# Clustered attention and a mixture of causal-attention experts in one program: a second emission order for the same recorded operations

## The chip, the cores and the metric

The kernel runs on one core of one Trainium2 chip. The metric is the device time of one launch in microseconds (us). Engines are named as in the profile: PE is the matrix engine (PEld are its weight loads), DVE the vector engine, ACT the scalar engine, POOL the GpSimd engine, and SP the engine that issues nearly all DMAs of this kernel.

## The reference

The first part is attention within clusters, for 4 batches of 8 heads, 768 positions and 64 dimensions. The second part takes the result as x (4 x 768 x 512), picks two of four experts for each position, and adds the experts' causal attentions with the weights of the gate.

```python
q_n = q / (np.linalg.norm(q, axis=-1, keepdims=True) + 1e-06)      # k_n, c_n alike
q_assign = np.argmax(np.einsum('bhsd,hcd->bhsc', q_n, c_n), axis=-1)   # 16 clusters; k_assign alike
mask = q_assign[:, :, :, None] == k_assign[:, :, None, :]
scores = np.where(mask, scale * np.matmul(q, k.transpose(0, 1, 3, 2)), -1000000000.0)
x = softmax(scores) @ v                     # heads side by side: (4, 768, 512)
...
logits = x @ w_gate                         # 4 experts, the 2 largest kept, softmax over them
for e in range(E):
    q, k, v = x @ wq[e], x @ wk[e], x @ wv[e]
    a = softmax(np.where(causal, -1000000000.0, scale * (q @ k.transpose(0, 2, 1))))
    ye = a @ v @ wo[e]
    out += (weight of e at this position, 0 if not picked) * ye
```

## The kernel before

The work is cut into 24 steps. The first 16 are head pairs of the first part (4 batches by 4 pairs); the last 8 are expert pairs of the second part (4 batches by 2 pairs). In time the first part fills about 0 to 400 us, with the second part's first steps overlapping its end.

A head pair runs as follows. k, q and v are loaded; PE transposes k and q (L516) and multiplies them with the normalized centroids (L547); DVE finds the cluster of each position and writes it as a row of zeros and ones (L559 to L567); from these come "rows" that are appended to the operands of the score matmuls, so that pairs of different clusters get a large negative score. Operands are split into a rounded part `hi` and a rest `lo = x - hi` to keep precision, and both are carried by DMA into the tiles `tk` (k side) and `tq` (q side). Score maxima come from matmuls at L1055 and DVE reductions at L1061; their negatives, `mr`, also go by DMA into `tq`. Scores (L1134 to L1143) are exponentiated by ACT (L1153); PE multiplies them with v (L1191). The sums of the softmax are collected by POOL or DVE: elementwise sums of 128x768 tiles (L375 on POOL, L376 on DVE), and then a matmul with ones (L1215). The sums `ssb` make a round trip through DRAM: `sd<-ssb`, `r<-sd`, a reciprocal on DVE (L1243), `rd<-r`, and `rb<-rd`, which spreads them over 64 partitions. With `rb` the result is normalized into `xt` (L1266) and stored as x.

An expert pair runs alike, with projections of x (L773, L813; copies by ACT at L819 and L820), the gate on DVE (L834 to L842, with one exponential on ACT at L844 and the rest at L848 to L852), causal maxima (L970 to L986), exponentials (L1017) and the out projection (L1305).

Every engine executes its instructions in the order in which they were emitted, and all transfers named here stand in the one queue of SP, issued at L358. An instruction that waits holds up everything behind it on its engine. The order is neither that of the Python loops nor chosen by a scheduler at run time: all 3726 operations are first recorded in a `Plan`, and `Plan.run` emits them in the order of a table of numbers, `SEQ`; a letter behind a number moves the operation to the other engine that can do it (a: ACT, d: DVE, p: POOL). `SLOT` says which of the buffers of a name each tile takes. The durations that stand in the `op(...)` calls are not used when the program is emitted.

```python
        for word in SEQ.split():
            i = int(word.rstrip("adp"))
            o = self.ops[i]
            eng = self.LETTER.get(word[-1], o.eng)
            ...
            o.ways[eng][1]()
```

While PE has no work at the start, 37 calls of `spin` (placed by `SEQ` as well) issue matmuls whose result nobody reads, at L1332 and L1327. I call them fillers.

Of the kernel before, what the change touches and what calls it, by code (L numbers as in the profile page):

```python
# [10 lines left out]
def _warn_once_fixed(msg, *args, **kwargs):  # L11
# [26 lines left out]
418 5 25 3 7 24 64 13 6 20 22 32 21 18 34 16 30 10 40 45 41 46 49 50 51 52 53 37 38 42d 55 43 47 56 57 19 1 29 27  # L38
231 234 232 233 222 227 223 12 228 394 69 44p 48p 70 246 68 67 39 58 59 235d 60 61 225d 0 36 62 63 66 65 26 28 395
77 78 79 224 226p 31 71 11 237 4 33 229 230p 238 239 8 80 81p 14 9 397 82p 403 17 399 401 73 84 396 72 74 83 54 76p  # L40
75p 566 249 85 398p 400 402p 23 2 88 15 96 108 94 92 35 240 241 109 97 104 242 243 89 421 93 404 405 406 407 106 244
245 247 422 248 100 409 410 90 102 86 105 101 111 114 115 107 87 95 136 256 103 257 134 98 173 174 99 91 110 163 164
168 169 157 158 252 137 253 152 116 117 138 153 112 113 254 255p 258 260 261 250 423 575 259p 262 135 139 130 131
# [3 lines left out]
302 265 292 293 279 280 303 290 291 430 431p 426 432 427p 434 433 236 251 184 185 189 182 183 310 195 196 188 190  # L47
193 199 267 268 273 202 311 277 278 203 308 309 207 208 204 578 579 266 300 306 296 283 284 194 210 211 274 307 301
287 297 312 313 314d 315 447 448 460 461 445 576 577 437 438 468 449 446 450 457 469 472 571 572 573 567 568 439 440
435 473 436 209 212 213 178 179 581 474 475 453 454 569 570p 574p 478 353 479 470 471 458 582 583 584 585 354 339  # L50
# [3 lines left out]
605 379 380 480 377 319 466 320 481 467 484 321 328d 376d 333d 338d 343d 347 348 378 381 742 743 744 745p 738 739  # L54
740 741p 349 350 382 945 923 459 485 631 628 629 486 487 749 645 620 635 747 646 750 383 909 218 219 748 633 616 617
639 612 613 634 621 636 351 352d 752 753 384 503 649 385 386 954 763 387 765 764 650 651 754 652 632 640 501 546 516
# [3 lines left out]
514 766 767 768 770 771 772 773p 774 946 656 657d 658 947d 775 388 389 1116 580 507 521 522 505 510d 548d 769 776  # L60
552 553 554 555 948d 951d 952 390 972 674 675 802 803 804 785 786 805 779 789 955 956 780 665 666 667 957 958 659
810 811 824 795 796 825 799 800 790 814 815 679 787 680 960 961 515 520 523 524 556 557 962 781 782 662 816 817 677
678 660 818 819 696 687 661 688 663 777 664 788 963 964 698 668 699 700 669 822 697 670 672 673 701 682 783 720 721
702 703 715 716 965 784 823 966 778 808 683 722 812 806 807 809 813 820 710 821 826 723 967 968 689 690 797 798 953p
949p 973 971 712 713 1117 1121 791 1122 792 793 671 1125 751 558 974 975 391 676 681 684 685 794 801 717 707 708 970
969 1287 559 392d 705 718 978 979 976d 1118d 980 686d 981 704d 706 709d 982 983 827 692 693 711 725 726 977 828d 829
560 561 221 562 564 563 984 833 1003 839 1128 1129 840 834 841 1126 991 1123 1124p 1119d 1142 714d 719d 724d 727
691d 694 1127d 1131 1132 1028 835 1004 695d 728 1120 1296 729 1144 565 922 992 843 844 1022 1023 1029 830 1032 1033
# [137 lines left out]
        "7301746154621553250067046341503275432707130341722002261416574140212631230256766304524377512365417302",  # L206
    vt="010101010101010100101100001110",
    mx="0101010110011001010110101010100101010101",
    ssb="010101010101010101101010",
    acc="010101010101011010011001101010011010",  # L210
    avu="010101010101010101100110",
    r="0101010101010101010101010",
    xt="0100110010110001010011100101000111011",
# [1186 lines left out]
```

## Time and profile before

| | |
|---|---|
| three timed runs, us | 683.66, 685.24, 685.85 (median 685.24) |
| profiled execution, us | 684.16 |
| its span, us | 682.3 |
| busy: PE | 666.6 us (98%) |
| busy: DVE | 518.4 us (76%) |
| busy: POOL | 355.1 us (52%) |
| busy: ACT | 341.0 us (50%) |

The span reaches from the first to the last recorded instruction; the profiled execution took 1.9 us more than it. The profiled execution lies 1.08 us under the median of the timed runs. A PE that is "busy" may have matmuls in flight behind each other, so 98% is not 98% of its peak. The granted clock of PE was 1.00 in every stretch shown below.

### The profile page before, as it was taken

To read this page: it belongs to the slowest core of one execution; us is meant where nothing else is said; L and a number is where in the kernel's file an instruction comes from. 1 tells how busy PE (TensorE), PEld (TensorE's weight loads), DVE (VectorE), ACT (ScalarE), POOL (GpSimd) and SP (SyncE) were. 2 spreads that over 40 slices of the span, in tenths; PEclk is the share of its full clock that TensorE was granted. 3 is DMA by queue.
4 is the path that set the end of the run, shared out by engine and by line. 5 is a ranking of instruction groups with operands and counts; after the bars stand their busy time and mean duration, and the time that the engine had idled before them with its cause. 6 is when DMAs were issued, how large, how long until landed. Compare 5 with 4: busy or idle time off the path is not lost.

```text
span 682.3 us, 13483 instructions
## 1 busy us (share of the span) xinstructions
PE 666.6 (98%) x4831; PEld 519.2 (76%) x4831; DVE 518.4 (76%) x1179; ACT 341.0 (50%) x789; POOL 355.1 (52%) x308
## 2 busy tenths in 40 slices
PE   8999999899999999999999999999899999999998
PEld 6777588477686677687686688969879979868976
DVE  6997779789896898889988966666856588656462
ACT  4556466356464475464684553254334434424613
POOL 7496476153888764753578467148431322642200
PEclk9999999999999999999999999999999999999999
DMA  6877757777667768658576631413011130114123
GB/s 187 209 195 170 181 131 176 202 177 202 163 162 205 175 183 205 153 152 220 141 192 163 172 104 48 118 57 110 24 55 42 49 83 30 57 41 141 47 73 124
DMA packets 70734, 90.78 MB, mean 133 GB/s; under 512 B 21088, under 2 KB 60428, under 8 KB 70668
## 3 DMA queue, kind: packets, MB, share of 16 engines
q1 hardware_dynamic: 70524, 89.90, 49.8%
q8 instruction: 38, 0.62, 0.4%
q14 instruction: 28, 0.23, 0.1%
q10 hardware_dynamic: 144, 0.03, 0.0%
HBM read 36.54 MB, written 12.91 MB: 72 GB/s over the span
## 4 chain that ended last, share of the span: by engine, by line
PE 84%; DVE 5%; DMA 4%; POOL 2%; SPq 2%; ACT 1%; issue 1%; POOLq 0%; DVEq 0%; ACTq 0%
PE banks L1191 19%; PE banks L773 10%; PE banks L1055 9%; PE banks L1134 8%; PE banks L1135 7%; PE banks L1003 6%; PE banks L813 5%; PE banks L1305 5%; PE banks L1215 2%; PE banks L516 2%; PE banks L970 2%; PE banks L547 2%; SPq L358 2%; PE banks L1138 1%; PE banks L1143 1%; POOL wvh L375 1%
## 5 line engine op out<-in xcount | busy, mean ns | idle before, releaser
L1061 DVE TENSOR_REDUCE mx<-banks 128x1 f32<-128x384 f32 x384 | 190.0, 548 | 18.9 <-PE banks L1055 17.9
L1055 PE MATMUL banks<-tk,tq 80*128 80x384 f32 x384 | 112.4, 359 | 2.5 <-DVE avu L371 1.1
L1134 PE MATMUL banks<-tq,tk 128*128 128x384 f32 x324 | 113.4, 350 | 0.0
L1135 PE MATMUL banks<-tq,tk 97*128 97x384 f32 x324 | 109.7, 339 | 0.0
L1055 PEld LDWEIGHTS banks<-tk,tq 80*128 80x128 f32 x384 | 68.3, 189 | 13.9 <-issue 4.4
L1153 ACT ACTIVATE p<-banks 128x384 f32<-128x384 f32 x144 | 65.8, 498 | 25.1 <-PE banks L1135 15.8
L1134 PEld LDWEIGHTS banks<-tq,tk 128*128 128x128 f32 x324 | 61.3, 189 | 4.3 <-issue 0.6
L1135 PEld LDWEIGHTS banks<-tq,tk 97*128 97x128 f32 x324 | 61.6, 190 | 0.0
L375 POOL TENSOR_TENSOR acc<-acc,p 128x768 f32<-128x768 f32 (+1 forms) x25 | 43.7, 1746 | 30.9 <-DVE M L1065 9.8
L978 DVE CUSTOM_DVE_ANT_0 banks<-banks,tri 128x384 f32<-128x384 f32 (+4 forms) x96 | 46.0, 529 | 10.7 <-PE banks L970 10.3
L1191 PE MATMUL banks<-p,vt 128*64 128x384 f32 x288 | 50.2, 490 | 0.0
L370 ACT ACTIVATE avu<-banks 128x384 f32<-128x384 f32 x35 | 16.9, 489 | 64.9 <-PE banks L1191 59.5
L375 POOL TENSOR_TENSOR lo<-xk,hi 128x384 fp32r<-128x384 f32 x28 | 28.4, 1026 | 36.3 <-DMA tq<-lo 22.7
L1153 ACT ACTIVATE xl<-banks 128x384 f32<-128x384 f32 x88 | 41.6, 498 | 8.1 <-PE banks L1135 5.6
L1003 PE MATMUL banks<-tk 64*128 64x384 f32 (+2 forms) x432 | 44.5, 312 | 0.0
L1153 ACT ACTIVATE xh<-banks 128x384 f32<-128x384 f32 x80 | 38.3, 499 | 7.9 <-PE banks L1135 7.3
L1266 POOL TENSOR_TENSOR xt<-avu,rb 128x384 f32<-128x384 f32 x28 | 28.3, 1021 | 23.6 <-DMA rb<-rd 23.6
L1191 PEld LDWEIGHTS banks<-p,vt 128*64 128x64 f32 x288 | 20.1, 137 | 24.5 <-issue 21.3
L1003 PEld LDWEIGHTS banks<-tk 64*128 64x128 f32 x432 | 35.4, 185 | 1.6 <-ACT p L1017 0.5
L1191 PE MATMUL banks<-xl,vt 128*64 128x384 f32 x176 | 30.7, 488 | 0.0
L375 POOL TENSOR_TENSOR wvh<-wvh,p 128x768 f32<-128x768 f32 x13 | 24.3, 1866 | 11.6 <-DVE wvh L376 10.4
L1017 ACT ACTIVATE tq<-banks 128x768 f32<-128x768 f32 (+2 forms) x41 | 26.4, 670 | 4.8 <-PE banks L1003 4.2
(322 smaller groups left out, 1682.0 us busy)
## 6 DMA issues: line engine op xcount, KB each, us to landing
tk<-hi SPq DMA_DIRECT2D x60, 192.0 KB
tq<-hi SPq DMA_DIRECT2D x56, 192.0 KB
rb<-rd SPq DMA_DIRECT2D x46, 192.0 KB
vt<-in_v_dram SPq DMA_DIRECT2D x16, 384.0 KB
x<-xt SPq DMA_DIRECT2D x16, 384.0 KB
kt<-in_k_dram SPq DMA_DIRECT2D x15, 384.0 KB
qt<-in_q_dram SPq DMA_DIRECT2D x15, 384.0 KB
tk<-lo SPq DMA_DIRECT2D x30, 192.0 KB
```

Source lines behind the costliest of these rows:

```text
L375: ways = [("pool", t_pool(n), lambda: POOL.tensor_tensor(dst(), a(), b(), op=fn)), ("dve", t_dve(n), lambda: DVE.tensor_tensor(dst(), a(), ...
L773: PE.matmul(m()[:, :HW], w_()[:, dc, es], x_[dc]()[:, js], start=(i == 0), stop=(i == 3 * DC - 1))
L813: PE.matmul(m()[:, :NV], x_[dc]()[:, ts], w_()[:, dc, :], start=(i == 0), stop=(i == 3 * DC - 1))
L978: DVE.tensor_tensor_reduce(ps()[:, h, :w], ps()[:, h, :w], tri[:, 512 - w:], 1.0, -3.0e38, OP.add, OP.max, to)
L1003: PE.matmul(p()[:, h, o_:HW], kone[0][r] if a is None else a()[r, ks], b()[r, qs], start=(j == 0), stop=(j == 3))
L1055: PE.matmul(ps()[:, :w], Q[0:R, 0, h, c * 128:(c + 1) * 128], K[0:R, 0, h, i * w:(i + 1) * w], start=True, stop=True)
L1061: DVE.tensor_reduce(mx()[:, h, cc, i:i + 1], ps()[:, :w], axis=AX.X, op=OP.max)
L1134: PE.matmul(p()[:, o_:HW], K[:, 1, h, ks], Q[:, 1, h, qs], start=True, stop=False)
L1135: PE.matmul(p()[:, o_:HW], K[0:R, 0, h, ks], Q[0:R, 0, h, qs], start=False, stop=True)
L1153: ACT.activation(pt()[:, h, po:po + w], p()[:, o_:HW], AF.Exp, scale=SC)
L1191: PE.matmul(av()[h * 64:(h + 1) * 64, o_:HW], d["vv"](h, kc), pt()[:, h, po:po + HW - o_], start=(kc == 0), stop=(kc == nk - 1), tile_posi ...
L1305: PE.matmul(m()[:, :n1 - n0], a_()[:, ts], w_()[:, ep, n0:n1], start=(ep == 0 and i == 0), stop=(ep == EP - 1 and i == 2))
```

## The change

The operations that are recorded, the buffers and the transfers stay. What differs is the table `SEQ` (all of it), the tables `SLOT` for ten of the names, the planner's numbers in the `op(...)` calls of DMAs (which the emission does not use), and `spin`:

```diff
@@ SEQ
-418 5 25 3 7 24 64 13 6 20 22 32 21 18 34 16 30 10 40 45 41 46 49 50 51 52 53 37 38 42d 55 43 47 56 57 19 1 29 27
...
+23 15 64 0 14 5 4 32 28 40 45 46d 47d 48p 41 43 27 6 37 38 42d 49 50 51 52 1 13 53 55 56 12 57 231 234 25 232 20 222
...
-        o = op("sp", 2 * [(0.58, 1.05, 0.04)], go, t1 + 7, sums, [ssb])
+        o = op("sp", 2 * [(0.58, 1.05, 0.12)], go, t1 + 7, sums, [ssb])
...
-    filled = [0]
...
     def spin():
-        filled[0] += 1
-        if filled[0] in (22, 31):
-            a, w = (identf, identf) if filled[0] == 31 else (blk[:, 0], blk[:, 1])
-            for i in range(8):
-                j, n = i % 6 * 66, 65 if a is identf else 66
-                PE.matmul(idle()[:, j:j + n], a, w[:, :n], start=True, stop=True)
-        elif filled[0] in (23, 32, 33):
-            pass
-        else:
-            for _ in range(2):
-                PE.matmul(idle()[:, :256], onesb, onesb[:, None, :].to_broadcast([128, 2, 128]), start=True, stop=True)
+        for _ in range(2):
+            PE.matmul(idle()[:, :256], onesb, onesb[:, None, :].to_broadcast([128, 2, 128]), start=True, stop=True)
```

So the fillers are 74 matmuls of 256 columns instead of 64 of these and 16 smaller ones. Ahead of the first transposes of k stand 16 of them, where 32 stood.

Counted over the whole program, the choice of engines moves too: sums of 128x768 are 118 on DVE instead of 95, and 96 on POOL instead of 119. The copies are split between ACT and DVE nearly as before.

The order moves nearly everywhere, by small steps. Three places are shown, with the rows of one engine each.

First, SP's queue where, in the trace of before, the time is about 118 to 136 us. The numbers behind a name tell tiles apart; `tk_98`, `tq_97` and `tq_99` are operand tiles of the scores. Before:

```order
L358 DMA qt_1514<-in_q_dram 128x2x384
L358 DMA vt_1516<-in_v_dram 128x2x384
L358 DMA sd<-ssb_1383 4x1x192 x2
L358 DMA tk_98<-rows_1483 16x4x384
L358 DMA tq_99<-rows_1483 16x4x384
L358 DMA kt_1540<-in_k_dram 128x2x384
L358 DMA r_1542<-sd 128x12
L358 DMA tq_99<-hi_1550 64x2x384 x4
L358 DMA tq_97<-mr_1595 1x12x128
L358 DMA rd<-r_1542 128x12
...
L358 DMA rb_1602<-rd 64x768 x2
L358 DMA tq_99<-lo_1555 64x2x384 x2
```

and the same step of the program after the change:

```order
L358 DMA sd<-ssb_1344 4x1x192 x2
L358 DMA qt_1354<-in_q_dram 128x2x384
L358 DMA tk_98<-hi_1302 64x2x384 x4
L358 DMA vm_1332<-in_moe_wq_dram 128x4x64
L358 DMA tk_98<-lo_1365 64x2x384 x2
L358 DMA r_1509<-sd 128x12
...
L358 DMA tq_99<-hi_1535 64x2x384 x4
L358 DMA rd<-r_1509 128x12
L358 DMA tq_97<-mr_1550 1x12x128
L358 DMA tq_99<-lo_1547 64x2x384 x2
L358 DMA vt_1562<-in_v_dram 128x2x384
L358 DMA rb_1611<-rd 64x768 x2
```

The store `sd<-ssb` moved ahead of the load of q, the load of v moved behind the whole piece, eight DMAs instead of three stand between `sd<-ssb` and `r<-sd`, and `tq<-lo` moved ahead of `rb<-rd`.

Second, ACT's queue at the first gate of the second part (about 482 to 491 us before). L844 is the exponential of the gate; L1017 are exponentials of scores. Before:

```order
L1017 ACTIVATE tq_5474<-banks 128x2x256
L1017 ACTIVATE p_0_5484<-banks 128x2x128
L1017 ACTIVATE p_0_5484<-banks 128x2x256
L844 ACTIVATE sm_5503<-sm_5503 128x6
L1017 ACTIVATE tq_5474<-banks 128x2x128
L1220 ACTIVATE ssb_5540<-banks,eps 128x192
```

and after the change:

```order
L819 ACTIVATE lg_5376<-banks 128x4
L820 ACTIVATE vm_5378<-banks 128x256
L370 ACTIVATE tk_98<-banks 128x384
L844 ACTIVATE sm_5292<-sm_5292 128x6
L819 ACTIVATE lg_5376<-banks 128x4
L820 ACTIVATE vm_5378<-banks 128x256
```

L844 no longer stands among exponentials of scores; it moved some 26 instructions of ACT on, in between the copies of the next projections. The eleven small DVE instructions that it waits for (L834 to L842) stand after the change behind the last maximum of their step (L986), ahead of that step's next copies.

Third, DVE's queue at the start of the program. `xk` and `hi` are copies of the transposed k; the four lines behind them build constant masks; L559 begins the search for the first cluster. Before:

```order
L371 COPY xk_185<-banks 128x384
L1337 TENSOR_SCALAR acc_88<-acc_88 128x256
L1338 TENSOR_SCALAR acc_90<-acc_90 128x256
L1339 TENSOR_TENSOR blk<-acc_88,acc_90 128x256
L1340 TENSOR_SCALAR tri<-avu_75 128x128
L559 TENSOR_REDUCE sm_263<-banks 128x24
```

and after the change:

```order
L371 COPY xk_162<-banks 128x384
L371 CAST hi_164<-banks 128x384
L371 COPY xk_162<-banks 128x384
L1326 TENSOR_SCALAR acc_88<-acc_88 128x256
L1327 TENSOR_SCALAR acc_90<-acc_90 128x256
L1328 TENSOR_TENSOR blk<-acc_88,acc_90 128x256
L1329 TENSOR_SCALAR tri<-avu_75 128x128
L559 TENSOR_REDUCE sm_250<-banks 128x24
```

Two more instructions of 128x384 stand ahead of the masks and of L559.

## Rows read from the trace of the kernel before

**Rows 1.** First part of the page: span, and busy time of each engine.

```profile
span 682.3 us, 13483 instructions
PE 666.6 (98%) x4831; PEld 519.2 (76%) x4831; DVE 518.4 (76%) x1179; ACT 341.0 (50%) x789; POOL 355.1 (52%) x308
```

**Rows 2.** Windows: us; PE, PEld, DVE, ACT, POOL busy; PE clock; DMA share; GB/s.

```profile
0.00:50.00 50.00, 46.75 (x332) 36.67 (x333) 42.53 (x100) 27.82 (x60) 36.26 (x49) 1.00 0.77 196
50.00:100.00 50.00, 48.61 (x336) 36.63 (x334) 40.63 (x89) 30.77 (x73) 29.64 (x20) 1.00 0.69 162
100.00:150.00 50.00, 46.09 (x307) 31.95 (x305) 40.73 (x80) 24.18 (x56) 22.97 (x16) 1.00 0.79 197
150.00:300.00 150.00, 149.28 (x1011) 109.27 (x1008) 127.85 (x263) 88.14 (x211) 104.77 (x71) 1.00 0.69 176
300.00:350.00 50.00, 48.85 (x336) 37.00 (x334) 44.55 (x87) 30.53 (x77) 23.72 (x21) 1.00 0.73 186
350.00:400.00 50.00, 49.98 (x325) 35.50 (x326) 44.18 (x92) 29.37 (x72) 32.57 (x24) 1.00 0.58 153
...
450.00:500.00 50.00, 48.24 (x407) 42.07 (x404) 34.75 (x93) 20.61 (x42) 29.10 (x31) 1.00 0.21 65
```

**Rows 3.** The same view, of the ten us with the largest gap.

```profile
130.00:140.00 10.00, 6.09 (x47) 3.41 (x44) 6.67 (x11) 3.42 (x8) 3.11 (x3) 1.00 0.81 209
```

**Rows 4.** SP's timeline, 119 to 135 us: start, us of issuing, transfer, count.

```profile
119.46 1.14 SPq L358 DMA_DIRECT2D sd<-ssb  x2
...
122.07 0.53 SPq L358 DMA_DIRECT2D kt<-in_k_dram  x1
125.34 0.35 SPq L358 DMA_DIRECT2D r<-sd  x1
...
133.60 1.33 SPq L358 DMA_DIRECT2D tq<-lo  x2
```

**Rows 5.** Chain of waits, 115 to 140 us: start, us, transfer.

```profile
120.07 5.25 DMA sd<-ssb
...
134.30 4.35 DMA tq<-lo
```

**Rows 6.** DVE's timeline, 132 to 139 us: [idle before <- what ended it].

```profile
132.05 0.56 DVE L371 CAST hi<-banks 128x384 fp32r<-128x384 f32 x1 [3.71 <-DMA tq<-hi]
132.53 2.93 DVE L376 TENSOR_TENSOR wvl<-wvl,xl 128x768 f32<-128x768 f32 x3
...
138.74 0.56 DVE L376 TENSOR_TENSOR lo<-xk,hi 128x384 fp32r<-128x384 f32 x1 [1.21 <-DMA tq<-lo]
```

**Rows 7.** PE's timeline, the same stretch.

```profile
135.51 0.53 PE L1215 MATMUL banks<-wvl,ones 128*32 128x192 f32 x8 [2.18 <-DVE wvl L376]
...
139.82 0.45 PE L1055 MATMUL banks<-tk,tq 80*128 80x384 f32 x1 [0.76 <-DVE mx L1061]
```

**Rows 8.** ACT's, DVE's and PE's timelines at the first gate, 485 to 491 us.

```profile
490.10 0.21 ACT L844 ACTIVATE sm<-sm 128x6 f32<-128x6 f32 x1 [5.97 <-DVE sm L842]
...
485.24 0.18 DVE L836 TENSOR_TENSOR oh<-oh,ramp 128x24 f32<-128x24 f32 x1
...
485.67 1.59 DVE L838 TENSOR_TENSOR oh<-oh,sm 128x24 f32<-128x24 f32 x1
...
490.63 0.44 PE L773 MATMUL banks<-xh,wkh 128*128 128x384 f32 x1 [1.70 <-ACT tq L1017]
```

**Rows 9.** Groups by line and shape: busy us, mean ns | idle before.

```profile
L375 POOL TENSOR_TENSOR acc<-acc,p 128x768 f32<-128x768 f32 x23 | 42.2, 1834 | 30.9 <-DVE M L1065 9.8 <-DVE acc L376 8.8 <-ACT wkl L1153 6.2
...
L376 DVE TENSOR_TENSOR acc<-acc,p 128x768 f32<-128x768 f32 x10 | 9.5, 955 | 0.3
```

**Rows 10.** DVE's timeline, the start of the program.

```profile
7.12 0.56 DVE L371 COPY xk<-banks 128x384 f32<-128x384 f32 x1 [1.09 <-PE banks L516]
...
10.70 0.56 DVE L559 TENSOR_REDUCE sm<-banks 128x24 f32<-128x384 f32 x1 [0.27 <-PE banks L554]
```

**Rows 11.** Windows of the fillers' line alone (columns: PE, PEld, clock, DMA share, GB/s).

```profile
4.50:6.20 1.70, 1.70 (x18) 1.48 (x15) 1.00 0.95 345
```

More of the change, by code (lines that the diff above doesn't have):

```diff
@@ L62 @@
[L62 to L66, printed above, removed]
@@ new lines @@
+2543 2528 2529 2665p 913p 2672 2848 2673 2270 2271 943 944p 2303 2304 2305 2684 2327 2306 2683 2536 2537 2546 2547
+2452 2565 2566 2462 2459 2559 2463 2453 2419 2534 2560 2535 2406 2407 941 2555 2556 2420 2408 2443 2444 937 915p
+2412 2413 2674 2424 2675 2460 2425 2414 2447 2538 2539 2571 2464 2465 2572 2676 2415 2431 2416 2417 2448 940p 938p
+2139 942p 2140 2426 2427 2544 2449 2545 2434 2450 2435 2429 2421 2422 2432 2563 2564 2677 2678 2553 2554 2557 2409
+2410 2411 2430 2526 2532 2558 2533 2679 2680 2577 2540 2457 2458 2445 2454 2455 2467 2686 2469 2573 2541 2527 2548
@@ L207 @@
[L207 to L213, printed above, removed]
+    ps="03214576521507523076243214501423501340035327472473425561733470441636243132117104315012062536207124475727"
+        "11670164450560654321267575376706630675103233262154332524171602477107037277557521646515202071376070055252"
+        "06146657075607344637332071044142726761241442373377023326135146174550475300567362372715423444607356231611"
+        "07063125145052310134565650250122451522046454723776572253563312166553077567373776723001140647514523200606"
+        "32024065633527054566316612226270422217135145730135244141525521432550457250246017260024261705671447177673"
+        "50447201075563663023355142217737577306451455012502173072370016006671434065020224456450217003546515713052"
+        "44027260757721333550312741060161423134655554170762264314617045246033403101371662066055377410364336064316"
+        "07011016053570446150656104270707732452226164220166455177213312460074613405434106514560763724410734576353"
+        "23137200051266322270272533062417063143777446654727621213104340757660515550322760273411244653667320514206"
+        "50152305765237417102533035607040241117407611660221725662750157364130415675022414224275062107163631126362"
+        "5221456070425717650420635775001064423431075532062442746051706340176234765213203054630775721675460321",
@@ L214 @@
+    vt="010101011010101011011100010110",
+    mx="0110100110101010101001010110010101010101",
+    ssb="010101010101010101010101",
+    acc="010101010101010101010110011010011001",
+    avu="010101010101010101011010",
+    r="0101010101010101010110010",
+    xt="0100010101010101010101100110100110100",
     mr="01010101010101010101010",
@@ L602, in attention_operands @@
             free = [op("pool", 2.7, lambda: clear_rows(n % 3), t0 - 60)]
-        need_row = [op("sp", [(0.6, 2.15, 0.84)], place_rows(Q, 0), c2 + 8, [o_r] + free, [rows]),
-                    op("sp", [(0.6, 2.15, 0.84)], place_rows(K, 1), c2 + 8.2, [o_r] + free, [rows])]
+        need_row = [op("sp", [(0.6, 2.15, 0.5)], place_rows(Q, 0), c2 + 8, [o_r] + free, [rows]),
+                    op("sp", [(0.6, 2.15, 0.5)], place_rows(K, 1), c2 + 8.2, [o_r] + free, [rows])]
         need_row2, half_row = [], [need_row[:], need_row[:]]
@@ L615, in go @@
                     dma(T[dst_rows, slot, :, c], src()[r])
-            return op("sp", len(pars) * [(0.65, 2.3, 0.96)], go, due, after + free, use)
+            return op("sp", len(pars) * [(0.65, 2.3, 0.88)], go, due, after + free, use)
         low, high = slice(0, D), slice(D, 128)
@@ L669, in move @@
             def move(dst, src, due, after, use=()):
-                return op("sp", [(0.65, 2.1, 0.96)], lambda: dma(dst, src()), due, after, use)
+                return op("sp", [(0.65, 2.1, 0.88)], lambda: dma(dst, src()), due, after, use)
             need_st += q_lo[::2] + [move(Q[high, 1, :, :HW], lambda: Q[low, 0, :, :HW], c2 + 14, need_row[-2:])]
@@ L685, in weights @@
         W[nm] = use = [tmp(x, shape, FR) for x in (("s", "rows") if nm == "wo" else (nm + "h", nm + "l"))]
-        lds = [op("sp", [(0.59, 2.5, 0.96) if nm != "wo" else (0.59, 3.6, 1.7)], lambda sl=sl, ap=ap: dma(raw()[sl], ap), due,
+        lds = [op("sp", [(0.59, 2.5, 0.8) if nm != "wo" else (0.59, 3.6, 1.7)], lambda sl=sl, ap=ap: dma(raw()[sl], ap), due,
                   use=[raw], at=45.0)
@@ L863, in go @@
             dma(gd[0], gr())
[L864 removed]
+        o = op("sp", [(0.42, 1.0, 0.18)], go, t0 - 12, [o], [gr])
         g, g_ready = [], []
@@ L1088, in go @@
                     dma(qm()[0:65:64] if moe else Q[MR:MR + 1, 0].rearrange("p h s -> p (h s)"), mr())
-                o = op("sp", [(0.84, 1.14, 0.04)], go, due + 0.5, [o] + (d["zero"] if moe else sets_free(n)), [mr, qm] if moe else [mr])
+                o = op("sp", [(0.84, 1.14, 0.15)], go, due + 0.5, [o] + (d["zero"] if moe else sets_free(n)), [mr, qm] if moe else [mr])
                 m_ops = 2 * [2 * [[o]]]
```

294 lines of the change are left out of this document (141 added, 153 removed), and 38 rows, old and new, of the table SEQ.

## The prediction

> **What bounds the kernel now.** I read the page's busy times first, then windows of fifty microseconds, then the timelines where PE has a gap, and last the groups by line for the price of each kind of instruction.
>
> PE is busy for 666.6 of 682.3 us [rows 1], so its gaps sum to 15.7 us; no other engine is above 76%. The change adds and removes no useful matmul. So it can gain only in those gaps (and in lulls that the records hide, since a PE that is counted busy may still have a thin stretch), and it can lose anywhere. The windows say where the gaps are [rows 2]: 3.25 us in the first fifty, which is the start; 1.39 in 50 to 100; 3.91 in 100 to 150; 0.72 in the 150 us after that; 1.15 in 300 to 350; 0.02 in 350 to 400; and 1.76 in 450 to 500, where the second part computes its first gate. The 3.91 us are all in one piece of ten microseconds, 130 to 140 [rows 3]: 10 minus 6.09.
>
> **What happens at 130 to 140.** SP issues the store `sd<-ssb` at 119.46 and, two short transfers and a load of k later, reaches `r<-sd`, which may not be issued before the store has landed. The load of k was issued by 122.60; `r<-sd` goes out at 125.34 [rows 4]. For 2.74 us SP does nothing, and everything behind it waits: the four `tq<-hi`, `tq<-mr`, `rd<-r`, `rb<-rd`, `tq<-lo`. The chain of waits names the store's landing, 5.25 us, and then that of `tq<-lo`, 4.35 us [rows 5]. DVE stands 3.71 us until `tq<-hi` has left its source buffer, so the sums behind that cast are late; it stands another 1.21 us for `tq<-lo` [rows 6]. PE waits 2.18 us for the sum `wvl` and 0.76 us for a maximum that DVE then delivers late [rows 7]. The DMA engines are 81% busy in this stretch [rows 3], the highest share of the rows shown for the middle of the program, which is why a small store needs 5.25 us.
>
> **The change part by part.**
>
> *SP's order there.* The store now stands ahead of the load of q, the load of v is gone from in front of it, and eight transfers stand between it and `r<-sd`. What they take to issue: one DMA costs 0.5 to 0.65 us at SP (1.14 for the two of the store, 1.33 for the two of `tq<-lo`, 0.53 for the k load [rows 4]), so eight take about 4.9 us, against 5.25 for the landing. SP's wait of 2.74 us shrinks to at most half a microsecond, and the store should land sooner, with no load just ahead of it. `tq<-lo` no longer waits for the reciprocal's round trip either, since it is ahead of `rb<-rd`. I take the whole gap as gone: 3.9 us. If transfers land as late as now whatever the order, nothing is won here: the bounds are -3.9 and 0. I take the upper gain because the cause seen in the rows, a queue behind one wait, is exactly what is rearranged.
>
> *ACT's order at the first gate.* L844 sits in ACT's queue 5.97 us for DVE's gate, with an exponential of scores behind it; PE waits 1.70 us for that exponential [rows 8]. After the change L844 stands among copies of projections some 26 instructions on, so the exponentials pass. The gate's DVE chain is the same work. -1.7 us, bounds -1.7 and 0 (0 if the copies behind L844 now hold up PE equally).
>
> *DVE's order at the start.* Today DVE does one copy of 128x384, which ends at 7.68, then builds the masks, then starts L559 at 10.70 after an idle 0.27 us [rows 10]; it was busy until 10.43. Now two more such copies stand ahead. A copy or cast of this shape takes 0.56 us, and its follower starts 0.08 us before its end 132.05 + 0.56 against 132.53, [rows 6], so two cost 0.96 us: the masks end at 11.4, and L559 starts there instead of at 10.70. L559 is the head of the first pair's chain, on which PE waits at the start, so +0.7 us. Bounds: 0, if the q side ends later than the k side anyway, and +1.8, if those copies also wait for PE (another 1.09 us, the idle time ahead of the first copy [rows 10]), whose transposes of k are what they read.
>
> *Fillers.* Ten more of 256 columns and sixteen small ones fewer. 18 of them ran in 1.70 us [rows 11], so the ten cost about 1 us of PE, and the small ones gave back more than that. They lie in stretches in which PE has nothing to do. 0 us; if all ten stood in the way, +1 us.
>
> *Sums moved from POOL to DVE.* Twenty-three sums of 128x768 change the engine: 23 x 0.955 = 22 us more on DVE, 23 x 1.834 = 42 us less on POOL [rows 9]. DVE goes from 518 to about 540 us, POOL from 355 to about 313. They lie in the first part, eight stretches of fifty us, so DVE gets 2.75 us more in each. It has between 40.6 and 44.6 us in a stretch today [rows 2]; it would have at most 47.3. Does a busier DVE cost PE time? In the rows it does not: the stretch with 44.18 lost 0.02 us of PE, that with 44.55 lost 1.15, the lighter ones, with 40.63 and 42.62 per fifty, lost 1.39 and 0.24. I take 0. The upper bound is that every stretch loses what the worst of the heavy ones does, 8 x 1.15 = 9.2, in place of the 3.3 us that these stretches lose today besides the start and the piece at 130 us: +5.9. The lower bound: a POOL sum takes 1.9 times as long as one on DVE, so the results come sooner; if this removed all of the 3.3 us, it would be -3.3.
>
> The Trainium skill ("SBUF — State Buffer", section "Who interferes with whom") says that a DVE instruction with two inputs in SBUF contends with a GpSimd instruction that reads SBUF. The trace agrees: two 128x24 operations of DVE, neighbours in the gate, took 0.18 and 1.59 us [rows 8], the long one while POOL summed; no run here shows yet how often this hits the moved sums. By that rule a sum moved to DVE takes a partner away from POOL, and the sum would rather fall than rise.
>
> *Everything else.* The table moves almost every operation by a few places. That makes or removes small waits which no row of before can price; they go into the range.
>
> Sum, against the profiled execution: 684.16 - 3.9 - 1.7 + 0.7 = 679.3 us. The median of the timed runs is 1.08 us above the profiled execution, so for a median 680.3 us (679.26 + 1.08).
>
> **The rivals.**
>
> *A larger gain.* All the gaps of the middle go, 1.39 + 3.91 + 0.72 + 1.15 + 0.02 + 1.76 = 8.95 us [rows 2], and the start loses nothing of weight: 684.16 - 8.95 + 0.7 + 1.08 = 677.0 us. For it: the gaps are all waits of order, and no engine but PE is full. Against it: a new order has gaps of its own; in 150 to 300 the old one already runs with 0.72 us lost in 150.
>
> *DVE becomes the limit.* The upper bound of the moved sums comes true and eats the gain: 680.3 + 5.9 = 686.2 us, no change that can be told. For it: DVE would be at 47.3 of 50 in the heaviest stretch, with no slack for a late transfer. Against it: the row with 44.18 and a gap of 0.02. The Trainium skill ("Perfetto Trace Analysis", section "Optimizing Scalar/DVE Operations") warns that moving work between GPSIMD and DVE might not help, because they share a read port; no run here shows this for whole sums.
>
> *The same blockage elsewhere (slower).* The new order again puts a wait for a landing in SP's queue ahead of transfers for which PE waits. The price of one is known, 3.9 us of PE for 2.74 us of SP. Three later places of the new order have loads of q, k or v close ahead of a store `sd<-ssb` and its `r<-sd`. One blockage gives 684.2 us, which is no change; two give 688.1, which is slower. The decision falls where loads together with other traffic keep a store in the air longer than the transfers behind it take to issue, 0.6 us each: with five of them, over about 3 us. For it: DMA share is 0.69 to 0.79 in the stretches up to 350 us [rows 2], and the landing of a store has been 5.25 us once. Against it: of sixteen pairs in before only one shows a gap of this size.
>
> **How the numbers follow.** Less than 0.3% (2.06 us, 683.2 to 687.3 around the median) is about what a measurement of this kernel cannot tell from no change. My forecast, 680.3 with its own range of 677 to 683, gets 0.43. The larger gain gets 0.15. DVE as the limit gets 0.16, the blockage 0.26, of which 0.05 is a single one and 0.21 two or more. Faster is forecast plus larger gain, 0.58; same is DVE as the limit plus the single blockage, 0.21; slower 0.21. The range is 675 to 688.5: below, the larger gain with 2 us of thin stretches filled as well; above, two blockages. Outside I leave about 2 in 10, mostly three blockages or more, or gains of thin stretches beyond what gaps show.
>
> **What would show each step right or wrong.** The gap of PE around the step that now lies at 130 us should be under 0.5 us, with SP's `r<-sd` following its neighbours without a wait of more than 0.5 us. The idle time ahead of L844 should no longer end a wait of PE for L1017. L559 should first start near 11.4 us. DVE's busy time should be near 540, POOL's near 313 us. PE's busy time less fillers stays, and its gaps sum to about 10.8 us instead of 15.7. The prediction is wrong if PE waits for DVE sums (L376 into L1215) in many stretches at once, if SP stands for `r<-sd` several times, or if PE's busy time itself changes by more than the fillers, since then the gaps were not the place where time was lost.

## The result, and the profile after the change

The changed kernel takes 673.92 us (median of 673.12 to 675.14) beside 684.54 us of the kernel before on the same chip: 0.9845 of it, 95% interval 0.982 to 0.987. Run again as it is on two other chips it gave 0.9886 (0.9854 to 0.9917) and 0.9894 (0.9865 to 0.9922). Faster it is, then, as forecast, but the first figure lies 1.1 us under the range that I gave, 675 to 688.5, and 6.4 us under the 680.3 that I took for likeliest. On the two other chips the medians were 675.74 and 675.65 us, just inside the range. The profiled execution took 673.12 us.

The page of the changed kernel begins with its span and the busy times:

```profile
span 671.4 us, 13404 instructions
PE 663.9 (99%) x4817; PEld 513.6 (76%) x4817; DVE 543.4 (81%) x1210; ACT 340.1 (51%) x791; POOL 302.7 (45%) x275
```

PE's gaps sum to 671.4 - 663.9 = 7.5 us, where they were 15.7 [rows 1]; I had expected 10.8. PE's busy time fell too, by 2.7 us. The fillers account for about half of that (12.1 us of them, 13.3 before); the useful matmuls, as many as before, are counted busy 1.5 us less, and in which stretches is not shown. So of the 10.9 us of span some 8.2 were gaps; that PE's busy time changes by more than the fillers was one of my signs of being wrong. DVE is at 543 us (540 expected), POOL at 303 (313 expected). The windows, with the columns of [rows 2], show in which stretch the gaps went:

```profile
0.00:50.00 50.00, 47.58 (x327) 35.73 (x329) 44.03 (x103) 27.41 (x59) 35.72 (x49) 1.00 0.83 200
50.00:100.00 50.00, 49.98 (x341) 36.52 (x339) 46.16 (x92) 29.09 (x70) 28.32 (x19) 1.00 0.71 172
100.00:150.00 50.00, 49.44 (x336) 36.36 (x333) 44.95 (x94) 27.87 (x66) 30.04 (x21) 1.00 0.78 185
150.00:300.00 150.00, 149.82 (x1013) 109.27 (x1013) 133.62 (x270) 91.87 (x219) 76.07 (x52) 1.00 0.72 185
300.00:350.00 50.00, 49.93 (x341) 36.97 (x339) 47.88 (x98) 30.72 (x76) 31.35 (x25) 1.00 0.72 173
350.00:400.00 50.00, 49.74 (x326) 35.48 (x323) 44.84 (x83) 25.66 (x61) 21.97 (x21) 1.00 0.58 156
450.00:500.00 50.00, 49.87 (x434) 43.57 (x436) 39.78 (x111) 19.67 (x42) 19.71 (x24) 1.00 0.22 66
```

Every stretch from 50 to 350 us lost most of its gap, not only the two pieces that I had counted; 350 to 400 has a small new one, 0.26 us. Past the first fifty the DMA share stayed where it was, within 0.03. DVE now has 44 to 48 us of work in each fifty of the first part: in 300 to 350 it is busy for 47.88 us, and PE misses 0.07.

A second way to read the same: the 1056 matmuls of L1191 (probabilities times v) stand in the same sequence in both programs. This table, worked out from the traces, gives the start of the first transpose and of some of the 66th matmuls (us), for the two kernels and for two experiments that are told below:

```
               before   after         b_three        b_five
first L516       6.27    4.51 (-1.8)    4.55 (-1.7)    4.78 (-1.5)
L1191 no. 66    74.97   72.40 (-2.6)   72.71 (-2.3)   74.59 (-0.4)
no. 132        103.02  100.60 (-2.4)  101.90 (-1.1)  102.89 (-0.1)
no. 198        147.22  141.03 (-6.2)  145.21 (-2.0)  142.60 (-4.6)
no. 462        284.09  277.59 (-6.5)  281.79 (-2.3)  279.19 (-4.9)
no. 594        361.00  352.17 (-8.8)  358.19 (-2.8)  355.57 (-5.4)
no. 726        447.64  438.58 (-9.1)  444.75 (-2.9)  442.09 (-5.6)
no. 792        506.87  496.44 (-10.4) 501.98 (-4.9)  499.32 (-7.6)
no. 1056       669.45  658.49 (-11.0) 664.55 (-4.9)  661.87 (-7.6)
```

So the lead comes in steps: 1.8 us at the start, 3.8 between 103 and 147 us (the stall that I read first), 2.3 between 284 and 361, 1.4 between 448 and 507 (the gate), and 1.7 in all elsewhere. Where the kernel before lost its time between 284 and 361, its trace shows two waits:

```profile
288.62 0.62 PE L1055 MATMUL banks<-tk,tq 80*128 80x384 f32 x2 [0.61 <-DMA tq<-hi]
316.64 0.62 PE L1055 MATMUL banks<-tk,tq 80*128 80x384 f32 x2 [1.15 <-DVE avu L371]
```

At the stall [rows 3] the window is nearly full now, 9.89 of 10 us:

```profile
126.00:136.00 10.00, 9.89 (x76) 6.98 (x73) 9.79 (x18) 5.03 (x12) 3.42 (x4) 1.00 0.68 174
```

SP's timeline there (compare [rows 4]):

```profile
107.82 1.26 SPq L358 DMA_DIRECT2D sd<-ssb  x2
...
115.53 0.59 SPq L358 DMA_DIRECT2D r<-sd  x1
...
122.98 2.87 SPq L358 DMA_DIRECT2D tq<-hi  x4
...
127.55 1.28 SPq L358 DMA_DIRECT2D tq<-lo  x2
```

and DVE's (compare [rows 6]):

```profile
125.31 3.00 DVE L376 TENSOR_TENSOR wvl<-wvl,xl 128x768 f32<-128x768 f32 x3
...
130.09 0.55 DVE L371 CAST hi<-banks 128x384 fp32r<-128x384 f32 x1
```

`r<-sd` follows its neighbours without a wait, as expected. But `tq<-hi` still goes out late. What is new is DVE's order: the three sums `wvl` now stand ahead of the cast of `hi` that needs that transfer, where they stood behind it [rows 6]. I had not looked at DVE's order there.

At the start the two events that I had forecast:

```profile
4.51 0.84 PE L516 MATMUL banks<-identf,kt 128*128 128x128 f32 x6
...
9.32 0.56 DVE L559 TENSOR_REDUCE sm<-banks 128x24 f32<-128x384 f32 x1
```

L516, the transposes of k, starts at 4.51 us where it started at 6.27. L559 starts at 9.32 us, not at 11.4 as I had said and not at 10.70 as before [rows 10]. At the gate ACT runs L844 in passing, with no idle time ahead of it (compare the 5.97 us of [rows 8]):

```profile
489.99 0.22 ACT L844 ACTIVATE sm<-sm 128x6 f32<-128x6 f32 x1
```

And the groups of sums, as in [rows 9]; the prices of one are nearly the same (1.87 us on POOL, 0.96 on DVE):

```profile
L375 POOL TENSOR_TENSOR acc<-acc,p 128x768 f32<-128x768 f32 x16 | 29.9, 1868 | 34.0 <-DVE acc L376 32.6 <-ACT p L1153 1.0
...
L376 DVE TENSOR_TENSOR acc<-acc,p 128x768 f32<-128x768 f32 x17 | 16.2, 956 | 6.1 <-POOL acc L375 5.2
```

### The profile page after: what moved, and what is told of

Its sections match the earlier page's. It is cut to its first block, busy times and chain, and to the rows that moved or that the text cites. A ratio compares the mean times of both kernels' runs of the same rounds, so it can differ in the third digit from the quotient of the medians.

```text
span 671.4 us, 13404 instructions
## 1 busy us (share of the span) xinstructions
PE 663.9 (99%) x4817; PEld 513.6 (76%) x4817; DVE 543.4 (81%) x1210; ACT 340.1 (51%) x791; POOL 302.7 (45%) x275
## 4 chain that ended last, share of the span: by engine, by line
PE 87%; DVE 10%; issue 1%; ACT 1%; POOL 1%; DVEq 0%; ACTq 0%
PE banks L1191 19%; PE banks L773 10%; PE banks L1055 10%; PE banks L1134 8%; PE banks L1135 8%; PE banks L1003 6%; PE banks L813 5%; PE banks L1305 5%; DVE acc L376 3%; PE banks L516 3%; PE banks L1215 2%; PE banks L970 2%; DVE mx L1061 2%; PE banks L1138 1%; PE banks L1143 1%; PE banks L547 1%
## 5 line engine op out<-in xcount | busy, mean ns | idle before, releaser
L1191 PE MATMUL banks<-p,vt 128*64 128x384 f32 x288 | 50.0, 490 | 0.0
L375 POOL TENSOR_TENSOR acc<-acc,p 128x768 f32<-128x768 f32 x16 | 29.9, 1868 | 34.0 <-DVE acc L376 32.6
L1191 PEld LDWEIGHTS banks<-p,vt 128*64 128x64 f32 x288 | 19.8, 137 | 24.6 <-issue 21.2
L375 POOL TENSOR_TENSOR wvh<-wvh,p 128x768 f32<-128x768 f32 x12 | 21.9, 1824 | 20.6 <-DVE wvh L376 19.7
L1191 PE MATMUL banks<-xl,vt 128*64 128x384 f32 x176 | 30.8, 488 | 0.0
L370 ACT ACTIVATE tk<-banks 128x384 fp32r<-128x384 f32 x16 | 7.8, 491 | 42.8 <-PE banks L773 42.8
```

The costliest lines, as they stand in the source:

```text
L375: ways = [("pool", t_pool(n), lambda: POOL.tensor_tensor(dst(), a(), b(), op=fn)), ("dve", t_dve(n), lambda: DVE.tensor_tensor(dst(), a(), ...
L1191: PE.matmul(av()[h * 64:(h + 1) * 64, o_:HW], d["vv"](h, kc), pt()[:, h, po:po + HW - o_], start=(kc == 0), stop=(kc == nk - 1), tile_posi ...
```

## The experiments

Two theories. *Waits add up*: the gain is the sum of a few waits of PE, each made by one instruction that stood too early or too late in one queue, so that each can be taken from the kernel before, or given back to the changed one, by a local edit. *Sums on DVE*: the gain comes from the moved sums, each shorter by 0.9 us, everywhere a little. A third is that it is spread over the whole order and no small set of edits shows it. The tables `SLOT` were not changed by themselves in any run. All runs of a group lie beside runs of the kernel before on the same chip, and ratios are taken to those. Where the edit is in the table of the order, the diff shows the rows that it moves.

### The changed kernel with one thing put back

```diff
 a_fill32, PE:                          a_gate_old, ACT:
-16 x L1321 MATMUL (fillers)           +L844 ACTIVATE sm<-sm 128x6
+32 x L1324 MATMUL (fillers)            ... (some 20 instructions)
 L516 MATMUL (transposes of k)         -L844 ACTIVATE sm<-sm 128x6
 a_sp_old, SP:
-L358 DMA sd<-ssb 4x1x192 x2
-L358 DMA qt<-in_q_dram 128x2x384
 L358 DMA tk<-hi 64x2x384 x4
 ...
 L358 DMA tk<-lo 64x2x384 x2
+L358 DMA qt<-in_q_dram 128x2x384
+L358 DMA sd<-ssb 4x1x192 x2
 L358 DMA r<-sd 128x12
 ...
+L358 DMA rb<-rd 64x768 x2
 L358 DMA tq<-lo 64x2x384 x2
 L358 DMA vt<-in_v_dram 128x2x384
-L358 DMA rb<-rd 64x768 x2
 a_sums_old: 48 sums of 128x768 DVE -> POOL, 25 POOL -> DVE, order unchanged
```

> The changed kernel with 32 fillers instead of 16 ahead of the first transposes of k, as before had them; nothing else differs. Theory 'waits add up' (the gain is the sum of the PE waits that the new order took away, one of them the fillers that stand in front of work that could start): the first L516 moves from 4.51 us back to about 6.3, and the kernel is 1.5 to 1.8 us slower (+0.25%). Rival 'sums on DVE' (the gain comes from the shorter sums): the start is slack, less than 0.5 us slower.

> The changed kernel with SP's order around 108 to 130 us put back: the store of the sums behind four hi, one weight, two lo and the load of q, and rb ahead of lo. The load of v stays where it is. If the place of the store alone makes the stall that before showed at 130 us, PE loses 3 to 4 us there again. If the stall needs what stood ready behind the wait (in the changed kernel the next transfers of SP wait until 119 us for their sources anyway), less than 1 us is lost.

> The changed kernel with the exponential of the first gate (L844) put back in ACT's queue directly behind the emission of DVE's gate, ahead of the exponentials and copies that now precede it. Waits add up: PE waits again about 1 to 2 us near 475 us, +0.2%. Rival (the gate's chain on DVE is elsewhere in the order now, so ACT is not held): within 0.3 us.

> The changed kernel's order with the engines of before for the 128x768 sums: 48 sums go from DVE to POOL, 25 from POOL to DVE. Waits add up with the sums at nothing, as forecast: within 2 us. Rival 'sums on DVE': most of the 10.6 us is lost again, +5 to +10 us. That an order searched for one split fits another badly speaks for some loss in either case.

Measured: 0.9882 (0.9853 to 0.991), 0.989 (0.9853 to 0.9926) and 0.9878 (0.984 to 0.9915) for the first three; the changed kernel as it is gave 0.9886 and 0.9894 on two other chips (no such control ran on this one). Put back singly, none of the three makes a difference that the times can show. The traces show them small: the first L516 at 6.60 us instead of 4.51, 1.0 us of it left at the first L554 (10.81 us against 9.73 and 9.79 in the other two); 1.1 us at the gate (PE waits 0.49 and 0.35 us near 473 us, which the changed kernel's profile does not show); and 0.8 us behind SP's piece. This last is the more telling one, since SP did stand again:

```profile
116.48 1.15 SPq L358 DMA_DIRECT2D sd<-ssb  x2
120.38 0.34 SPq L358 DMA_DIRECT2D r<-sd  x1
```

It waited 2.75 us from 117.63 on, as long as in the kernel before (2.74), and in the stretch that follows PE missed 0.12 us; the 0.8 us come later, when DVE waits 3.30 us for the next pair's `r<-sd`:

```profile
127.00:137.00 10.00, 9.88 (x76) 6.99 (x73) 9.79 (x18) 5.02 (x13) 0.78 (x1) 1.00 0.76 176
```

The wait of a queue had no price of its own. The view of what SP waits for says so for the whole program. Of before, then of after (us in total, times, longest):

```profile
SPq L358 <- DMA sd<-ssb: 21.4, 15, 2.6
```

```profile
SPq L358 <- DMA sd<-ssb: 25.8, 18, 3.7
```

SP stands longer for that store in the faster kernel than in the slower one.

The split of the sums put back: 1.0503 (1.0472 to 1.0534), 44 us slower than the changed kernel; neither theory had expected so much. The three costliest waits of PE in its trace are waits for sums:

```profile
PE banks L1215 <- DVE acc L376: 6.1, 2, 3.7
PE banks L1215 <- POOL wvh L375: 5.5, 2, 5.1
PE banks L1215 <- POOL acc L375: 3.6, 3, 1.3
```

This fits *sums on DVE*, but also an order that holds only for its own split; the reverse edit tells.

### The kernel before with one thing from the changed one

```diff
 b_fill16, PE:                         b_gate_new, ACT:
-32 x L1332 MATMUL (fillers)          -L844 ACTIVATE sm<-sm 128x6
+16 x L1332 MATMUL (fillers)           ... (18 instructions)
 L516 MATMUL (transposes of k)        +L844 ACTIVATE sm<-sm 128x6
 b_sp_new, SP:
-L358 DMA qt<-in_q_dram 128x2x384
-L358 DMA vt<-in_v_dram 128x2x384
 L358 DMA sd<-ssb 4x1x192 x2
+L358 DMA qt<-in_q_dram 128x2x384
 ...
-L358 DMA rb<-rd 64x768 x2
 L358 DMA tq<-lo 64x2x384 x2
+L358 DMA rb<-rd 64x768 x2
+L358 DMA vt<-in_v_dram 128x2x384
 b_sums_new: 48 sums of 128x768 POOL -> DVE, 25 DVE -> POOL, order unchanged
```

> The kernel before with the first sixteen filler calls cut to one matmul each: 16 instead of 32 fillers ahead of the first transposes, nothing else changed. Waits add up: the first L516 starts near 4.5 instead of 6.27 us; 1 to 1.8 us faster (-0.2%). Rival (the start waits for DVE's masks or for the centroids anyway): within 0.5 us.

> The kernel before with one piece of SP's order as after the change, around 118 to 136 us: the store of the sums ahead of the loads of q and v, the load of v behind lo, lo ahead of rb. Waits add up: the gap of PE of 3.9 us at 130 to 140 goes, -3.5 us (-0.5%). Rival (the stall needs more than SP's order to go, since the landing of hi also holds DVE): at most -2 us, with DVE still waiting for hi.

> The kernel before with the exponential of the first gate (L844) moved in ACT's queue to just ahead of the instruction that needs it, 18 rows on. Waits add up: PE's wait of 1.70 us for L1017 at 490 us goes, -1.5 us (-0.2%). Rival: ACT then waits elsewhere, within 0.5 us.

> The kernel before with the engines of the changed kernel for its 128x768 sums, in the order of before. Sums on DVE alone make the gain: -5 us or more. An engine split is worth something only in the order made for it: slower, +10 us or more, as the changed kernel was by 44 us with the split of before.

Measured: 0.9978 (0.9954 to 1.0003), 0.9935 (0.9913 to 0.9956), 0.9951 (0.9929 to 0.9973) and 1.0959 (1.0921 to 1.0997). The last refutes *sums on DVE*: the engines of the changed kernel make the kernel before 9.6% slower. In both directions the wrong split costs tens of microseconds. I take it that a sum then stands in a queue whose neighbours were ordered for something else; no run separates that. Part of the loss is PE's clock: its mean was 0.963 in the profile of b_sums_new and 0.980 in that of a_sums_old, which over their spans of 748.6 and 715.4 us makes an estimated 28 and 14 us.

The other three are waits that go. With L844 moved, the stretch around it is full (PE's gap of 1.70 us in [rows 8] lay ahead of 490.63 us; this program is 2.2 us ahead there):

```profile
485.00:490.00 5.00, 5.00 (x34) 5.00 (x33) 4.76 (x16) 0.00 (x0) 2.33 (x4) 1.00 0.24 76
```

With SP's piece in the new order `r<-sd` no longer waits, but DVE still does:

```profile
130.45 0.56 DVE L371 CAST hi<-banks 128x384 fp32r<-128x384 f32 x1 [1.76 <-DMA tq<-hi]
130.93 2.93 DVE L376 TENSOR_TENSOR wvl<-wvl,xl 128x768 f32<-128x768 f32 x3
```

PE waits 1.03 us for `wvl` and 0.43 for `acc` (2.18 and 0.43 before). SP's order was a part of that stall only; the cast in front of the sums is the other. Over the stretch from no. 132 to no. 198 of L1191 this program gains 2.9 us on the kernel before, the changed one 3.8.

In the run with fewer fillers the first L516 starts at 4.74 us, 1.5 us sooner, but by no. 198 the lead is gone (+0.2 us). The old stall is in place, and its trace shows a price that the profile of before did not have. The granted clock (last column but two) of the stretch of the stall and of the one behind it:

```profile
130.00:136.00 6.00, 2.66 (x20) 1.72 (x20) 4.15 (x6) 1.85 (x4) 0.00 (x0) 1.00 0.67 204
136.00:140.00 4.00, 3.79 (x22) 2.31 (x23) 2.64 (x7) 1.57 (x4) 3.24 (x3) 0.57 1.05 225
```

After 6 us in which PE worked for 2.66, it was granted the lower of its two levels for most of the next 4 us: with 0.57 as the mean, 4 x 0.43 / 0.5 = 3.4 us at half speed, 1.7 us lost. The profile of before had the same gap and kept its clock. The runs of the kernel before beside these had mean clocks of 0.989 to 0.999, and those with the lower clock were the longer ones: 681.7 to 686.1 us at 0.997 and above, 686.2 us and more at 0.993 and below. With SP's piece changed most had 1.000 or 0.999.

The times of single edits hold more than the edit. b_sp_new gains 0.65% or 4.5 us, and its trace 4.3 us against the trace of before; but only 2.9 of them lie at the stall. 1.7 us come between 284 and 361 us, where nothing was edited. b_gate_new gains 1.8 us there and b_fill16 2.0, all that is left of its lead at the end. The wait of 1.15 us at 316 us, which stands in the profile of before, is in none of these three traces: it comes and goes between executions of the old order.

### Several together, and how many fillers

```diff
 b_three = b_fill16 + b_sp_new + b_gate_new
 b_four  = b_three, and in SP's order near 60 us:
+L358 DMA kt<-in_k_dram 128x2x384
 L358 DMA sd<-ssb 4x1x192 x2
 ...
-L358 DMA kt<-in_k_dram 128x2x384
 a_fill8, PE:
-16 x L1321 MATMUL (fillers)
+8 x L1324 MATMUL (fillers)
 L516 MATMUL (transposes of k)
```

> The changed kernel as it is, beside the kernel before on another chip: a control for the runs that differ from it in one place. 0.982 to 0.987 of before.

> The kernel before with three local edits at once: 16 fewer fillers ahead of the first transposes, SP's piece at 118 to 136 us as after the change, L844 18 rows on in ACT's queue. The rest of the order and all engines stay. Waits add up: 0.22 + 0.65 + 0.49 = 1.36% as the three gave singly, ratio 0.986, nearly all of the changed kernel's gain. Rival (the gain is spread over the whole order, and the three overlap): ratio 0.990 to 0.993.

> As the one with three edits, and the load of k for the pair whose transposes wait at 71 us moved ahead of the store of the sums, some 5 us earlier in SP's queue. Waits add up: another 0.5 to 0.8 us, 0.1%, and the wait for kt at 71 us is gone. Rival (the load then delays the store and with it the round trip): no gain.

> The changed kernel with 8 instead of 16 fillers ahead of the first transposes. If the fillers in front are the limit there too, L516 starts at about 2.8 us or when k has landed (between 2.8 and 4.5), up to 1.5 us faster. If k lands at about 4.5 us anyway, or the first transposes then run at the lower clock for longer, nothing is gained, or up to 1 us lost.

Measured: 0.9886 for the control (a little above the 0.987 expected at most), 0.9922 (0.9895 to 0.995) for three edits, 0.9928 (0.9903 to 0.9954) for four, 0.9914 (0.9882 to 0.9946) for 8 fillers. Three edits, of thousands of moved operations, bring about two thirds of the gain, less than the 1.36% of the three singly. The fourth brings nothing: there is no wait for `kt` at 71 us (the trace of b_three has none either), and one of 1.98 us for `tq<-lo` stands at 81 us; no gain, as the rival had it. In the trace of b_three PE still waits 1.58 and 0.43 us for the sums at 133 us, with a clock of 0.57 over the next 4 us, so that its lead grows by only 0.9 us there; and 1.14 us at 314 us for a copy of `avu` that stands behind seven sums on DVE.

With 8 fillers PE waits for k itself:

```profile
4.39 1.51 PE L516 MATMUL banks<-identf,kt 128*128 128x128 f32 x6 [1.39 <-DMA kt<-in_k_dram]
```

Six transposes took 1.51 us (0.84 in the changed kernel's profile), the pace of the lower level, which here lasted until the fillers at 8.9 us; L554 came at 11.09 us, later than with 16 (8.73 to 9.79 us in six profiles). Sixteen end at 4.5 us, just behind k.

### What was left

```diff
 b_five = b_three, and in DVE's order near 132 us and 316 us:
-L371 CAST hi<-banks 128x384
 L376 TENSOR_TENSOR wvl<-wvl,xl 128x768 x3
 L376 TENSOR_TENSOR acc<-acc,xh 128x768
+L371 CAST hi<-banks 128x384
 ...
+L371 COPY avu<-banks 128x384
 L376 TENSOR_TENSOR wvh<-wvh,p 128x768 x2
-L371 COPY avu<-banks 128x384
 b_six   = b_five, and the last sum of wvh at 57 us on DVE instead of POOL
 a_three_old = a_fill32 + a_sp_old + a_gate_old
 a_best  = the changed kernel, one sum wvl<-p,p at 175 us on DVE instead of POOL
```

> The kernel before with the three edits, and three more at places where PE still waited for a sum or a copy: at 126 to 134 us four sums on DVE ahead of the cast of hi that waits for a transfer; at 309 to 316 us a copy of avu ahead of the last two sums on DVE; at 57 us the last sum of wvh on DVE instead of POOL. Waits add up: 1.5 + 0.4 + 1 + 0.5 us less than with three edits, ratio about 0.988, as the changed kernel. Rival (spread over the whole order): as with three edits, 0.992, the waits reappear beside.

> The changed kernel with the three places put back at once: 32 fillers in front, SP's order of before at 108 to 130 us, L844 early in ACT's queue. If the places still cost what their traces show one by one (1.0 + 0.8 + 1.1 us), 2.5 to 3.5 us slower than the control. If the new order has slack there, within 1.5 us. If the places were worth in it what they were worth in the kernel before, 5 to 8 us.

> The changed kernel with one sum of 128x768 (the first of wvl at about 175 us) on DVE instead of POOL, where DVE waits for it and PE then waits 1.0 us for a maximum behind it in some executions. Waits add up: that wait goes, 0.5 to 1 us faster than the control. Rival: DVE is late elsewhere, no change.

> The changed kernel as it is, control on the chip of these runs: 0.985 to 0.990 of before.

Measured: 0.9941 (0.9919 to 0.9963), 0.9972 (0.995 to 0.9993), 0.986 (0.9833 to 0.9886), and 0.9894 for the control.

*b_six* is slower than expected, and its trace puts that on its own sixth edit: DVE was busy with maxima, the sum came later there than on POOL, and PE waited 2.65 us instead of 0.57; the mean granted clock was 0.95 and 0.96 over 40 to 60 and 60 to 80 us.

```profile
58.60 0.87 PE L1215 MATMUL banks<-wvh,ones 128*32 128x192 f32 x8 [2.65 <-DVE wvh L376]
```

Without that edit:

> The kernel before with six edits without the sum at 57 us, which goes back to POOL. Waits add up: 2 to 4 us faster than with three edits, ratio 0.987 to 0.990, most of the changed kernel's gain. Rival (spread over the whole order): 0.992.

0.9896 (0.9865 to 0.9926), which is the changed kernel's 0.9886 and 0.9894 within the intervals. The stall is gone from the stretch of [rows 3]:

```profile
126.00:136.00 10.00, 9.96 (x75) 5.90 (x71) 9.36 (x18) 4.18 (x10) 0.00 (x0) 1.00 0.80 205
```

and DVE's and POOL's busy times are those of before, 517 and 355 us. The fifth edit, at 316 us, did not remove its wait: the copy of `avu` now comes in time, and PE waits for the maximum behind it instead.

```profile
311.74 0.61 PE L1055 MATMUL banks<-tk,tq 80*128 80x384 f32 x2 [1.25 <-DVE mx L1061]
```

So by the trace it is the other four edits that count, and with them the gain is recovered as far as times can tell (7.8 us in the medians; the changed kernel gained 7.7 beside each of its two controls, and 10.6 on the first chip); no sum changed its engine. No control ran on the chip of b_five, and in the traces it has 7.6 us of the changed kernel's 11.0, so that a rest that is spread over the order is not excluded.

*a_three_old*: put back together, the three places cost 6.1 us against the control (681.78 against 675.65 us), near the whole gain, though each alone cost nothing that could be told. The trace shows a gap that no single edit had. SP stands 3.4 us for a `lo` that POOL computes, `r<-sd` of the next pair stands behind that and goes out at 142.09 us (137.36 in the changed kernel, 140.95 with SP's piece alone put back), it takes 5.21 us to land, and DVE stands for it with everything behind it.

```profile
142.09 5.21 DMA r<-sd
```

```profile
147.32 0.23 DVE L1243 RECIPROCAL r<-r 128x12 f32<-128x12 f32 x1 [5.77 <-DMA r<-sd]
```

```profile
144.00:148.00 4.00, 2.55 (x15) 1.05 (x11) 0.68 (x3) 0.00 (x0) 3.84 (x3) 1.00 1.03 209
148.00:152.00 4.00, 3.90 (x13) 2.65 (x14) 3.67 (x8) 1.96 (x5) 3.87 (x4) 0.87 0.65 239
```

The same reciprocal waited 1.63 us in the changed kernel and 3.30 with SP's piece alone put back; with those two waits PE's gaps there came to less than 0.1 us, with 5.77 us it has one, and the lower clock follows it (0.87).

*a_best*: in both controls PE waits 1.0 us near 182 us for a maximum that stands on DVE behind a sum waiting for POOL:

```profile
182.45 0.28 PE L1076 MATMUL banks<-identf,M 128*12 128x128 f32 x1 [1.02 <-DVE M L1065]
```

With the first sum of that chain on DVE the wait is gone from the trace, and the runs took 673.67 to 674.95 us, median 674.38, against 674.54 to 679.65 of the control, median 675.65. It is the fastest version on that chip, by about the 1 us of the wait. That the edit did it is not shown: the two intervals overlap, and the first profile of the changed kernel and that of a_sp_old do without this wait too.

## Why the prediction was wrong

Two terms of the sum failed: the start, for which I wrote +0.7 us with the fillers at 0, and "everything else", which I left out of the sum. The two other terms, the stall and the gate, came out in the trace.

*The start: the step that failed in sign.* I costed the fillers at nothing because "they lie in stretches in which PE has nothing to do", and gave the start +0.7 us for DVE's two copies. The row was in my hands: 18 fillers ran from 4.50 to 6.20 us [rows 11], directly ahead of the transposes, and k lands at 4.39 us (a_fill8). Sixteen fewer let the first transpose start 1.8 us sooner, and the copies that I had charged to DVE then ran in time that DVE had spent idle, its 1.09 us of [rows 10]. The row of L559 said too that it waited for PE (0.27 us for L554), and not for the masks. The lead at the first transposes was -1.8 and at L559 -1.4, not +0.7. What that is worth at the end is not shown as well: singly 0.22% (b_fill16), about 1.5 us, with an interval that just reaches no change and a trace in which the lead is lost again by 147 us; and a_fill32 could not be told from the changed kernel.

*The other gaps: the step that was left out.* 1.39 us at 50 to 100 and 1.15 us at 300 to 350 stood in [rows 2], and I left them to the range as "everything else". They went: 0.8 us of lead up to the first sixteenth of L1191, 2.3 us between 284 and 361 (of which PE had waited 0.61 us at 288 and 1.15 at 316). That was my rival of a larger gain: 677.0 us, and with the start right (-1.8 in place of +0.7) 674.5 us. In the traces that rival held; I gave it 0.15. But it had luck on its side: the wait at 316 us is missing from four traces of the old order that were not edited there (b_fill16, b_sp_new, b_gate_new, b_four), so the one profile of before held more gap than many executions do.

*The stall at 130 us: right in size, half right in cause.* -3.9 forecast, -3.8 in the trace. But SP's order alone brought 2.9 us in the trace; the sums had also to be ahead of the cast (b_five: 4.5 us from no. 132 to no. 198). The cause that I gave for the store's 5.25 us, a DMA share of 0.81, was read from 130 to 140 us, when the store had landed; while it was in the air, from 119.5 to 125.3 us, the share was 0.97. In b_sp_new, with the loads of q and v no longer ahead of it, `r<-sd` went out 3.7 us after the store's first issue instead of 5.9, at a share of 0.80; whether the share or the loads made the difference is not shown. And the price that I put on "one blockage", 3.9 us of PE for 2.74 us of SP, is no price: the changed kernel has 25.8 us of such waits, and a_sp_old's 2.75 us cost 0.8. I take it that what stands ready behind the wait, and how soon PE needs it, decides; no run varies that by itself. The rival of blockage elsewhere came true on SP and cost nothing, except when three edits together made a late landing hold up DVE (a_three_old).

*The gate: right.* -1.7 forecast, -1.4 in the trace; L844 moved by itself gives 2.0 us there (b_gate_new).

*The moved sums: right at nothing.* DVE took on 25 us of work, and no gap of PE in the changed kernel's trace is larger than 0.41 us past the first 40 us. That the split has no worth by itself, and a large negative one in a foreign order, I had not said.

*Sum.* In the traces: -1.8 - 0.8 - 3.8 - 2.3 - 1.4, and the rest -0.9, is -11.0 us, where I had +0.7 - 3.9 - 1.7 = -4.9. Of the 6.1 us between them the start makes 2.5 and the gaps that I left out about 3. What stays open is how the gain splits in the medians. On the three chips it was 1.55, 1.14 and 1.06%. Part of it is clock that the kernel before loses in most executions: of the 31 beside the two controls only two kept a mean of 1.000, and these took 681.81 and 681.60 us, beside 674.5 to 675.6 of the changed kernel at that clock, which is 6 to 7 us. The profiled execution of before, with the same clock, took 684.16 us; so its trace may hold some 2.5 us of waits, perhaps those at 288 and 316 us, that these executions do not have.

## What to carry to other kernels

Price every gap of the engine that is the bound, also the small ones, and ask of each what stands in front of the late instruction in its own queue: here a few local edits were worth most, and by the times perhaps all, of a new order of 3726 operations. Read more than one execution before you price a gap: the one at 316 us was there in half of the traces of the old order only. Work that fills idle time is free only until the work that it fills for could start. A wait of a queue is not a cost by itself; the same 2.7 us went with a loss of 3.9 us in one order and of 0.8 us in another.

## What the runs showed of the hardware

PE's clock had a part in this that the one profile of before did not show. At the start the fillers of 256 columns went 0.215 us apart, which is 1.2 columns per ns and so the lower of PE's two levels (1.2 and 2.4 GHz), and then at twice the pace; the windows of the first microseconds give 1.00 all the same. The moment of change differed between executions that start alike: 4.5, 4.8 and 5.4 us in three profiles of the changed kernel, 6.6 to 6.7 in those of a_sp_old, a_gate_old and a_best. By that alone the first matmul of L1191 starts up to 1.1 us later. Behind the stall at 130 us the granted clock fell to the lower level for 3.4 us in the traces of b_fill16 and b_three, and not in those of before and b_gate_new, whose gaps there were no shorter than that of b_three. And it fell with no gap ahead of it: in both controls (here a_again) PE was busy without a break from 640 us on, and yet

```profile
640.00:650.00 10.00, 10.00 (x77) 7.02 (x76) 6.91 (x20) 3.21 (x8) 0.00 (x0) 1.00 0.25 84
650.00:661.00 11.00, 11.00 (x50) 8.35 (x51) 1.01 (x4) 1.19 (x2) 0.00 (x0) 0.53 0.32 108
```

which took 4.5 us of the lead in each. The profile of the first runs had 1.00 there. No run here shows why.
